# Attention with a maxout feed-forward on one core: the softmax of a chunk overlaps its neighbour, and the feed-forward has three result buffers

## The chip, the core and the metric

The kernel runs on one core of a Trainium2 chip. The metric is the device time of one execution in microseconds (us), as the median of three runs. The core's engines work side by side, each through its own list of instructions in the order of the program: TensorE (PE; its weight loads are PEld), VectorE (DVE), ScalarE (ACT), GpSimd (POOL), and SyncE (SP), which here issues nearly all DMAs. An instruction that waits for another engine holds up everything behind it on its own.

## The reference

Eight batches of 12 heads, 448 tokens, head width 64. Q and K are normalised, attention is computed, the heads are put side by side to rows of 768, and a maxout feed-forward follows. All is float32.

```python
q_n, k_n = rmsnorm(q, g_q), rmsnorm(k, g_k)          # x / sqrt(mean(x*x) + 1e-6) * g
scores = np.matmul(q_n, k_n.transpose(0, 1, 3, 2)) / 8
attn = np.exp(scores - np.max(scores, axis=-1, keepdims=True))
attn = attn / (np.sum(attn, axis=-1, keepdims=True) + 1e-09)
x = np.matmul(attn, v)                               # (8, 12, 448, 64)
x = x.transpose(0, 2, 1, 3).reshape(3584, 768)
h = np.maximum(np.maximum(x @ w1, x @ w2), x @ w3)   # three 768 x 768 weights
out = h @ w_out
```

## The kernel before, in words

To keep float32 accuracy with 16-bit matmuls, every operand is split into an upper float16 part and a lower one (what the upper leaves over), and each product is three matmuls: upper x upper, upper x lower, lower x upper (`TERMS`).

**Groups, chunks, beats.** A group `g` is one batch and two heads: 48 groups, six to a batch. The 448 queries of a group are done in four chunks of 112. The program is written out in beats: a group has 12, `beat(g, i)`, three to a chunk (`c, part = divmod(i, 3)`). Each engine's order is the order in which the beats emit instructions. `later(n, work)` puts work off by n beats; `tick()` at a beat's end emits what is due.

**A chunk of softmax.** `scores` (L469) makes six matmuls into `sc`, a PSUM tile of two banks (one for each head), of which two exist. `softmax` has VectorE take the maximum of each row (L480) and scale it to `nm` (L482); ScalarE then takes the two exponentials in place, with their sums (L486). `upper_weights` makes the reciprocal sums `rs` on VectorE (L496, L500) and the normalised upper parts `pp` on ScalarE (L503). `lower_weights` makes the lower parts on VectorE (L513), which is the last reader of `sc`. `turn_weights` transposes `pp` into `pt` by a DMA (L523). When a group's four chunks are turned, `add_values` (L539) multiplies by V in the next group's beats, and `finish` (L548 on ScalarE, L549 on VectorE) writes the result's two parts `xt`, the feed-forward's input.

**The work around it.** For the groups ahead, beats load Q, K and V (SP), square and sum them (GpSimd L332, VectorE L338), scale them (GpSimd L345 to L383), split them (`upper_rows` on ScalarE L394, `lower_rows` on GpSimd L401) and transpose them (`turn_rows`, L409); V is scaled and split in `scale_v`, `upper_v`, `lower_v`.

**The feed-forward.** When a batch is finished, its feed-forward is queued, and `thirds(n)` takes n thirds from the queue in each beat, by the table `THIRDS`. A third is three matmuls. The first layer (`layer1`, L563, 18 products of six thirds) accumulates into `acc`; `hidden` empties it: the first of three products is copied to `m` (ScalarE L574), the second and third are merged with it by a maximum (VectorE L578), and after the third the result is split into the parts of `ht` (ScalarE L584, VectorE L588). The second layer (`layer2`, L627, six or eight products) accumulates likewise, and `result` (ScalarE L636) copies it to `osb` for the store. All these `acc` come from the pool `ps_m` with two buffers of one bank.

**Decoding.** In the first ten groups the weights arrive as 64-bit floats, and a block of them is decoded every five beats (`prep_block`): ScalarE on `raw` (L171), VectorE on `d_f` (L179, L183, L188, L155), then `largest` finds the block's largest value with two small matmuls into the PSUM tile `marks` (L142, L149) and a maximum `top` (L144) between them; `w_top` (L242) follows from it.

Of the kernel before, what the change touches and what calls it, by code (L numbers as in the profile page):

```python
# [12 lines left out]
ALU = mybir.AluOpType  # L13
# [21 lines left out]
def qknorm_attention_maxout_ffn_kernel(  # L35
# [53 lines left out]
    ps_a = ctx.enter_context(tc.tile_pool(name="ps_a", bufs=1, space=bass.MemoryType.PSUM))  # L89
    ps_m = ctx.enter_context(tc.tile_pool(name="ps_m", bufs=2, space=bass.MemoryType.PSUM))  # L90
    ps_b = ctx.enter_context(tc.tile_pool(name="ps_b", bufs=1, space=bass.MemoryType.PSUM))

# [43 lines left out]

    marks = ps_b.tile([P, 512], F32, name="marks")
    n_marks = [P]

    def largest(column, done):  # L140

        nc.tensor.matmul(marks[0:1, 0:P], column, ident, start=True, stop=True)  # L142
        top = sb.tile([1, 1], F32, name="top", bufs=2)
        nc.vector.tensor_reduce(top, marks[0:1, 0:P], axis=AX, op=ALU.max)  # L144

        def spread():
            at = n_marks[0]
            n_marks[0] += 1
            nc.tensor.matmul(marks[:, at:at + 1], ones, top, start=True, stop=True)  # L149
            done(marks[:, at:at + 1])  # L150

        later(1, spread)

# [64 lines left out]
    def prep_block(n):  # L218
# [47 lines left out]

        later(3, lambda: largest(most, scale))

# [289 lines left out]
    def layer1(b, xs, hs, ft, j, keep):  # L558
        wt = w_sb[:, ft * NJ + j].rearrange("p a (c f) -> p a c f", c=NCT)
        acc = ps_m.tile([P, 512], F32, name="acc", tag="m")  # L560
        for c in range(NCT):
            for n, (wp, xp) in enumerate(TERMS):
                nc.tensor.matmul(  # L563
                    acc[:, :S], wt[:, wp, c], xs[c][:, xp],
                    start=(c == 0 and n == 0), stop=(c == NCT - 1 and n == 2),
                )
            yield
        later(0, lambda: hidden(b, acc, hs, ft, j, keep))

    def hidden(b, acc, hs, ft, j, keep):  # L570
        top = w_top[:, ft, j:j + 1]
# [9 lines left out]
        if j == 2:  # L581
            ht = sb.tile([P, 2, S], F16, name="ht", bufs=6)
            by = h_down[:, ft:ft + 1]
            nc.scalar.activation(ht[:, 0], most, AF.Copy, scale=by)  # L584
            hs.append(ht)

            def lower():
                nc.vector.scalar_tensor_tensor(  # L588
                    out=ht[:, 1], in0=most, scalar=by, in1=ht[:, 0],
                    op0=ALU.mult, op1=ALU.subtract,  # L590
                )
                odd = (b % 2) * LEFT
                nc.gpsimd.tensor_copy(hx[:, ft, :, odd:odd + LEFT], ht[:, :, 3 * P:S])  # L593

            later(1, lower)

# [22 lines left out]
    def layer2(b, hs, tk, half, box):  # L619
# [4 lines left out]
        for f in range(NFT):  # L624
# [6 lines left out]
            yield  # L631
        later(0, lambda: result(b, acc, osb, tk, half))

# [86 lines left out]

    THIRDS = (2, 3, 2, 2, 3, 2, 1, 1, 2, 2, 3, 2)

    def beat(g, i):
        w, n = g - 1, g + 2
        c, part = divmod(i, 3)
        if g < G and part == 0:
            scores(g, c)
            softmax(g, c)
        if g < G and part == 2:
            upper_weights(g, c)  # L730
        if w >= 0 and i == 6:
            add_values(w)
        thirds(THIRDS[i] + (len(queue) > 1 and i % 6 == 4))
        if w >= 0 and i == 8:
            finish(w, x_of[w // NP])
        if w >= 0 and i == 10 and g % NP == 0:
            queue.append(ffn(w // NP, x_of[w // NP]))

        if g + 1 < G:
            if i in (0, 3):  # L740
                upper_rows(g + 1, "kq"[i // 3])
            if i in (1, 4):
                lower_rows(g + 1, "kq"[i // 3])
            if i in (3, 6):
                turn_rows(g + 1, "kq"[i // 3 - 1])

        if n < G:
            if i in (0, 2):
                squares(n, "kq"[i // 2])
            if i in (2, 4):  # L750
                sum_squares(n, "kq"[i // 2 - 1])
            if i == 5:
                inv_rms(n)
            if i == 6:
                scale_k(n)
            if i == 8:
                scale_q(n)
# [4 lines left out]
        if 0 < g < G - 6 and i == 5:  # L762
            load_v(g + 6)
            later(4, lambda: largest_v(g + 6))
        if g == 1 and i == 0:
            bound_v(0)
        if g > 1 and g % NP == 0 and g < G and i == 1:
            bound_v(g // NP)
        if g == 1 and 3 <= i < 6:
            (scale_v, upper_v, lower_v)[i - 3](0)  # L770
        if 0 < g < G and i >= 9:
            (scale_v, upper_v, lower_v)[i - 9](g)

        if g + 3 < G:
            if i == 0:
                load_k(g + 3)
            if i == 2:
                load_q(g + 3)
        if i == 1 and w >= 0:
            turn_weights(w, 3)  # L780
        if g < G and i in (4, 7, 10):
            turn_weights(g, i // 3 - 1)
# [3 lines left out]
        tick()  # L786
        if g < G and part == 2:
            lower_weights(g, c)

    for g in range(G + 1):  # L790
        for i in range(12):
            beat(g, i)
# [35 lines left out]
```

## Time and profile before

| | before |
|---|---|
| median of 3 runs | 1409.9 us (1409.33 to 1411.42) |
| the profiled execution | 1410.49 us, span 1408.7 us, mean granted TensorE clock 0.915 |
| busy, share of the span | TensorE 75%, weight loads 35%, VectorE 62%, ScalarE 51%, GpSimd 51% |

The page counts an engine as busy while one of its compute instructions runs. Where no engine is near its full span, the time goes in waits between them, and the groups of instructions by line say how long each engine stood idle in front of one and what released it. The kernel has three stages: groups with decoding, groups without, and a last stretch in which only the feed-forward is left; shares over the whole span mix them.

### The profile page before, as it was taken

How to read it: one execution, taken by the hardware profiler on the slowest of the kernel's cores; microseconds unless marked ns; L12 is line 12 of the kernel's file. 1: busy time of each engine (PE TensorE's matmuls, PEld its weight loads, DVE VectorE, ACT ScalarE, POOL GpSimd, SP SyncE). 2: the span in 40 equal slices, each digit the busy share in tenths (PEclk: the TensorE clock that was granted, in tenths of full speed). 3: DMA queues.
4: the chain of work that ended last, by engine and by line, in shares of the span. 5: the costliest groups of instructions: out<-in, count | busy, mean ns of one | idle time of the engine just before them, and what ended most of it. 6: DMA issues, size and time to landing. Idle time of an engine off the chain costs nothing. (4 is left out here: it accounts for less than half of the span.)

```text
span 1408.7 us, 18557 instructions
## 1 busy us (share of the span) xinstructions
PE 1050.7 (75%) x6032; PEld 491.6 (35%) x6032; DVE 870.8 (62%) x1741; ACT 722.0 (51%) x1550; POOL 719.8 (51%) x759
## 2 busy tenths in 40 slices
PE   0334434768688888887888988888878989878998
PEld 0111111223234334433343434343433434334554
DVE  4777877778666666566656665666656665656120
ACT  2444445545455555555565565555555555555211
POOL 5575767744355546465564655555465555541000
PEclk9996556888899999999899999999999999999999
DMA  5765656655357565676565566655665657554201
GB/s 138 183 128 145 135 146 152 128 135 126 68 114 147 109 117 113 152 124 114 107 137 123 110 116 146 133 117 108 124 136 113 123 120 145 92 91 68 54 0 45
DMA packets 476800, 164.88 MB, mean 117 GB/s; under 512 B 423200, under 2 KB 472352, under 8 KB 476704
## 3 DMA queue, kind: packets, MB, share of 16 engines
q1 hardware_dynamic: 476176, 163.42, 56.4%
q8 instruction: 47, 0.77, 0.2%
q14 instruction: 49, 0.40, 0.1%
q10 hardware_dynamic: 528, 0.30, 0.1%
HBM read 51.97 MB, written 11.01 MB: 45 GB/s over the span
## 5 line engine op out<-in xcount | busy, mean ns | idle before, releaser
L563 PE MATMUL acc<-xt,w_sb 128*128 128x448 f16 x2592 | 559.7, 370 | 124.2 <-DVE ht L588 58.1
L486 ACT ACTIVATE sc<-sc,nm,down 112x448 f32<-112x448 f32 x384 | 267.8, 697 | 494.4 <-DVE nm L482 444.8
L563 PEld LDWEIGHTS <-w_sb 128*128 128x128 f16 x2592 | 253.0, 101 | 415.0 <-issue 223.7
L513 DVE SCALAR_TENSOR_TENSOR pp<-sc,rs,pp 112x448 f16<-112x448 f32 x384 | 244.7, 679 | 178.6 <-ACT pp L503 175.6
L503 ACT ACTIVATE pp<-sc,rs 112x448 f16<-112x448 f32 x384 | 223.2, 636 | 75.7 <-issue 46.2
L480 DVE TENSOR_REDUCE sc<-sc 112x2 f32<-112x896 f32 x192 | 209.1, 1089 | 8.5 <-PE sc L469 8.4
L469 PE MATMUL sc<-kt,qt 64*112 64x448 f16 x1152 | 171.4, 409 | 36.6 <-DMA qt<-qp 21.9
L627 PE MATMUL acc<-wo_sb,ht 128*128 128x384 f16 x864 | 153.1, 328 | 26.5 <-ACT osb L636 13.7
L401 POOL TENSOR_TENSOR kp<-kn,kp 128x512 f16<-128x512 f32 x48 | 56.8, 1183 | 185.6 <-ACT kp L394 185.6
L401 POOL TENSOR_TENSOR qp<-qn,qp 112x512 f16<-112x512 f32 x47 | 55.5, 1182 | 174.5 <-ACT qp L394 174.5
L539 PE MATMUL av<-pt,vp 128*64 128x448 f16 (+1 forms) x1152 | 136.8, 383 | 6.9 <-POOL vp L456 4.4
L349 POOL TENSOR_TENSOR ri<-ri,half_neg 128x15 f32<-128x15 f32 x48 | 135.4, 2822 | 4.0
L496 DVE TENSOR_SCALAR rs<-sc 112x2 f32<-112x2 f32 x192 | 30.0, 156 | 149.0 <-ACT sc L486 149.0
L627 PEld LDWEIGHTS <-ht 128*128 128x128 f16 x864 | 80.4, 98 | 94.9 <-issue 35.1
L142 PE MATMUL marks<-ident,w_row 128*1 128x128 f32 x48 | 12.6, 359 | 132.1 <-DVE w_row L155 128.6
L469 PEld LDWEIGHTS <-qt 64*112 64x112 f16 x1152 | 66.7, 139 | 117.8 <-issue 68.9
L456 POOL TENSOR_TENSOR vp<-vr,vp 128x448 f16<-128x448 f32 x48 | 51.3, 1069 | 90.2 <-ACT vp L450 89.7
L539 PEld LDWEIGHTS <-vp 128*64 128x64 f16 (+1 forms) x1152 | 61.1, 116 | 80.9 <-issue 47.6
L593 POOL COPY hx<-ht 128x128 f16<-128x128 f16 x48 | 14.0, 292 | 138.1 <-DVE ht L588 120.1
L442 POOL TENSOR_SCALAR vr<-vr,v_up 128x448 f32<-128x448 f32 x48 | 68.4, 1426 | 0.2 <-DVE v_up L435 0.2
L338 DVE TENSOR_REDUCE ss<-sq 128x7 f32<-128x448 f32 x96 | 61.2, 638 | 8.6 <-ACT sq L330 7.6
L366 POOL TENSOR_TENSOR qn<-qn,gain 112x512 f32<-112x512 f32 x47 | 61.1, 1301 | 3.7
(84 smaller groups left out, 1045.0 us busy)
## 6 DMA issues: line engine op xcount, KB each, us to landing
raw<-in_moe_w_dram SPq DMA_DIRECT2D x18, 768.0 KB, 4.5
qr<-in_q_dram SPq DMA_DIRECT2D x47, 224.0 KB, 3.4
kr<-in_k_dram SPq DMA_DIRECT2D x96, 96.0 KB, 2.7
vr<-in_v_dram SPq DMA_DIRECT2D x96, 96.0 KB, 2.7
raw<-in_moe_w_out_dram SPq DMA_DIRECT2D x6, 768.0 KB, 4.4
pt<-pp SPq DMA_TRANSPOSE x192, 3.8
out_dram<-osb SPq DMA_DIRECT2D x8, 336.0 KB, 2.9
out_dram<-osb SPq DMA_DIRECT2D x8, 288.0 KB, 3.3
```

The source lines that it names most:

```text
L338: nc.vector.tensor_reduce(sums[g % 2][:sq.shape[0], at], sq, axis=AX, op=ALU.add)
L349: nc.gpsimd.tensor_tensor(out=ri, in0=ri, in1=half_neg, op=ALU.pow)
L401: on.tensor_tensor(out=parts[:, 1], in0=n, in1=parts[:, 0], op=ALU.subtract)
L442: nc.gpsimd.tensor_scalar(out=vr, in0=vr, scalar1=v_up[:, g // NP:g // NP + 1], scalar2=None, op0=ALU.mult,)
L469: nc.tensor.matmul(sc[:QP, h, :S], qt[rows, qp, c], kt[rows, kp, KEYS[h]], start=n == 0, stop=n == len(TERMS) - 1,)
L480: nc.vector.tensor_reduce(low, sc[:QP, :, :S], axis=AX, op=ALU.max, negate=True)
L486: nc.scalar.activation(sc[:QP, h, :S], sc[:QP, h, :S], AF.Exp, bias=nm[:, h:h + 1], scale=down[:QP], accum_out=sc[:QP, 1, S + 8 + h:S + 9 ...
L503: nc.scalar.activation(pp[:, 0, h], sc[:QP, h, :S], AF.Copy, scale=rs[:, h:h + 1])
L513: nc.vector.scalar_tensor_tensor(out=pp[:, 1, h], in0=sc[:QP, h, :S], scalar=rs[:, h:h + 1], in1=pp[:, 0, h], op0=ALU.mult, op1=ALU.subtract,)
L539: nc.tensor.matmul(av[half, :S], vp[rows, group, vpart], pt[rows, 7 * wp + group], start=u == 0 and n == 0, stop=u == 3 and n == len(TERMS ...
L563: nc.tensor.matmul(acc[:, :S], wt[:, wp, c], xs[c][:, xp], start=(c == 0 and n == 0), stop=(c == NCT - 1 and n == 2),)
L627: nc.tensor.matmul(acc[:, :HW], lhs, wo_sb[:, f, wp, half * HW:(half + 1) * HW], start=(f == 0 and n == 0), stop=(f == NFT - 1 and n == 2),)
```

## The change

- `scores` of a chunk are emitted a beat earlier, in the last beat of the chunk before, ahead of that beat's thirds. In its own first beat the chunk's `softmax` comes first, and `lower_weights` of the chunk before come behind it. `upper_weights` move from the third beat to the second.
- The pool `ps_b` with its one bank goes; `ps_m` has three buffers, and each call of `largest` takes its `marks` tile from them. Its steps `reduce`, `spread` and `done` are now one beat apart.
- `hidden` runs a beat after its product is complete (for the last of a batch at once, as before), the upper part of `ht` a beat after that, and the lower part another; `result` runs a beat later.
- Other work of the beats moves by one or two beats, and one entry of `THIRDS` changes places.

The order on VectorE where the attention runs without decoding. Numbers behind a name tell the tiles of one name apart. Before:

```order
L496 TENSOR_SCALAR rs_5629<-sc_5579 112x2
L500 RECIPROCAL rs_5629<-rs_5629 112x2
L513 SCALAR_TENSOR_TENSOR pp_5632<-sc_5579,rs_5629,pp_5632 112x448 x2
L480 TENSOR_REDUCE sc_5648<-sc_5648 112x2
L482 TENSOR_SCALAR nm_5656<-sc_5648,down_132 112x2
L155 TENSOR_REDUCE v_rows_4685<-vr_5571 128x1
L549 SCALAR_TENSOR_TENSOR xt_5641<-av_5591,xt_5641 128x448
L578 SCALAR_TENSOR_TENSOR acc_5564<-acc_5564,w_top_100,m_5540 128x448
L588 SCALAR_TENSOR_TENSOR ht_5671<-acc_5564,h_down_102,ht_5671 128x448
```

The same chunks in the changed kernel:

```order
L494 TENSOR_SCALAR rs_5691<-sc_5658 112x2
L498 RECIPROCAL rs_5691<-rs_5691 112x2
L577 SCALAR_TENSOR_TENSOR acc_5592<-acc_5592,w_top_96,m_5580 128x448
L547 SCALAR_TENSOR_TENSOR xt_5706<-av_5629,xt_5706 128x448
L478 TENSOR_REDUCE sc_5710<-sc_5710 112x2
L480 TENSOR_SCALAR nm_5729<-sc_5710,down_128 112x2
L511 SCALAR_TENSOR_TENSOR pp_5694<-sc_5658,rs_5691,pp_5694 112x448 x2
L590 SCALAR_TENSOR_TENSOR ht_5709<-acc_5592,h_down_98,ht_5709 128x448
```

Before, the lower parts `pp` of a chunk (tile `sc_5579`) stand ahead of the next chunk's maximum (`sc_5648`); now the maximum of `sc_5710` and its `nm` stand ahead of the lower parts made from `sc_5658`. The two instructions on a third product, into `acc` and then `ht`, stood next to each other and are now four rows apart.

VectorE in a group with decoding; `d_f` is the block being decoded, `w_row`, `marks`, `top` and `w_top` lead to its largest value. Before:

```order
L188 SCALAR_TENSOR_TENSOR d_f_998<-raw_871,d_f_998 128x768
L155 TENSOR_REDUCE w_row_999<-d_f_998 128x1
L144 TENSOR_REDUCE top_1042<-marks_97 1x1
L496 TENSOR_SCALAR rs_1044<-sc_1014 112x2
L500 RECIPROCAL rs_1044<-rs_1044 112x2
L338 TENSOR_REDUCE ss0_87<-sq_1028 128x7
L242 TENSOR_SCALAR w_top_100<-marks_97 128x1
```

The same block in the changed kernel:

```order
L186 SCALAR_TENSOR_TENSOR d_f_997<-raw_871,d_f_997 128x768
L153 TENSOR_REDUCE w_row_998<-d_f_997 128x1
L494 TENSOR_SCALAR rs_1039<-sc_1001 112x2
L498 RECIPROCAL rs_1039<-rs_1039 112x2
L336 TENSOR_REDUCE ss0_84<-sq_1022 128x7
L478 TENSOR_REDUCE sc_1052<-sc_1052 112x2
L480 TENSOR_SCALAR nm_1069<-sc_1052,down_128 112x2
L511 SCALAR_TENSOR_TENSOR pp_1042<-sc_1001,rs_1039,pp_1042 112x448 x2
L143 TENSOR_REDUCE top_1066<-marks_1064 1x1
```

Before, `top` stood right behind `w_row`, which TensorE first has to turn. Now the sums, the next chunk's maximum and the lower parts stand between the two.

The diff, cut to its core:

```diff
-    ps_m = ctx.enter_context(tc.tile_pool(name="ps_m", bufs=2, space=bass.MemoryType.PSUM))
-    ps_b = ctx.enter_context(tc.tile_pool(name="ps_b", bufs=1, space=bass.MemoryType.PSUM))
+    ps_m = ctx.enter_context(tc.tile_pool(name="ps_m", bufs=3, space=bass.MemoryType.PSUM))
...
-    marks = ps_b.tile([P, 512], F32, name="marks")
-    n_marks = [P]
-
     def largest(column, done):
 
+        marks = ps_m.tile([P, 512], F32, name="marks", tag="m")
         nc.tensor.matmul(marks[0:1, 0:P], column, ident, start=True, stop=True)
         top = sb.tile([1, 1], F32, name="top", bufs=2)
-        nc.vector.tensor_reduce(top, marks[0:1, 0:P], axis=AX, op=ALU.max)
+
+        def reduce():
+            nc.vector.tensor_reduce(top, marks[0:1, 0:P], axis=AX, op=ALU.max)
 
         def spread():
-            at = n_marks[0]
-            n_marks[0] += 1
-            nc.tensor.matmul(marks[:, at:at + 1], ones, top, start=True, stop=True)
-            done(marks[:, at:at + 1])
-
-        later(1, spread)
+            nc.tensor.matmul(marks[:, P:P + 1], ones, top, start=True, stop=True)
+
+        later(1, reduce)
+        later(2, spread)
+        later(3, lambda: done(marks[:, P:P + 1]))
...
-        later(3, lambda: largest(most, scale))
+        later(4, lambda: largest(most, scale))
...
-        later(0, lambda: hidden(b, acc, hs, ft, j, keep))
-
-    def hidden(b, acc, hs, ft, j, keep):
+        gap = 0 if ft == NFT - 1 and j == NJ - 1 else 1
+        later(gap, lambda: hidden(b, acc, hs, ft, j, keep, gap))
+
+    def hidden(b, acc, hs, ft, j, keep, gap):
...
-            nc.scalar.activation(ht[:, 0], most, AF.Copy, scale=by)
             hs.append(ht)
+
+            def upper():
+                nc.scalar.activation(ht[:, 0], most, AF.Copy, scale=by)
+                later(1, lower)
...
-            later(1, lower)
+            later(gap, upper)
...
-        later(0, lambda: result(b, acc, osb, tk, half))
+        later(1, lambda: result(b, acc, osb, tk, half))
...
-    THIRDS = (2, 3, 2, 2, 3, 2, 1, 1, 2, 2, 3, 2)
+    THIRDS = (2, 3, 2, 2, 3, 2, 2, 0, 2, 2, 3, 2)
...
-        if g < G and part == 0:
-            scores(g, c)
-            softmax(g, c)
-        if g < G and part == 2:
+        k = 4 * g + c
+        if part == 0:
+            if g < G:
+                softmax(g, c)
+            if 0 < k <= 4 * G:
+                lower_weights(*divmod(k - 1, 4))
+        if part == 1 and g < G:
             upper_weights(g, c)
-        if w >= 0 and i == 6:
+        if part == 2 and k + 1 < 4 * G:
+            scores(*divmod(k + 1, 4))
+        if w >= 0 and i == 7:
             add_values(w)
         thirds(THIRDS[i] + (len(queue) > 1 and i % 6 == 4))
-        if w >= 0 and i == 8:
+        if w >= 0 and i == 10:
             finish(w, x_of[w // NP])
...
-        if 0 < g < G and i >= 9:
-            (scale_v, upper_v, lower_v)[i - 9](g)
+        if 0 < g < G and i == 9:
+            scale_v(g)
+        if 0 < g < G and i == 11:
+            upper_v(g)
+        if 0 < w and i == 0:
+            lower_v(w)
...
-            if i == 2:
+            if i == 1:
                 load_q(g + 3)
-        if i == 1 and w >= 0:
+        if i == 2 and w >= 0:
             turn_weights(w, 3)
-        if g < G and i in (4, 7, 10):
+        if g < G and i in (5, 8, 11):
             turn_weights(g, i // 3 - 1)
...
-        if g < G and part == 2:
-            lower_weights(g, c)
-
+
+    scores(0, 0)
     for g in range(G + 1):
```

Left out above: `upper_rows`, `lower_rows`, `turn_rows`, `squares`, `sum_squares`, `inv_rms`, `scale_k` and the first group's `bound_v` and `scale_v` stand one or two beats elsewhere.

## Rows read from the trace of the kernel before

**Rows 1.** Busy time by stretch: engines (instructions), granted clock, DMA share, GB/s.

```profile
125.00:158.00 33.00, 11.53 (x56) 4.84 (x56) 25.32 (x47) 17.25 (x34) 22.09 (x20) 0.55 0.59 133
...
400.00:1300.00 900.00, 757.18 (x4513) 354.70 (x4511) 560.75 (x1160) 513.87 (x1137) 484.76 (x531) 0.95 0.61 120
```

**Rows 2.** Timeline of ScalarE, line 548: start, us, engine, line, tiles, count.

```profile
82.12 0.54 ACT L548 ACTIVATE xt<-av 128x448 f16<-128x448 f32 x1
...
388.67 0.54 ACT L548 ACTIVATE xt<-av 128x448 f16<-128x448 f32 x1
...
1299.69 0.54 ACT L548 ACTIVATE xt<-av 128x448 f16<-128x448 f32 x1
```

**Rows 3.** Groups by line, 400 to 1300 us: busy, mean ns | idle before, releasers.

```profile
L486 ACT ACTIVATE sc<-sc,nm,down 112x448 f32<-112x448 f32 x292 | 203.6, 697 | 362.6 <-DVE nm L482 327.0 <-DVE v_down L431 13.2 <-DVE v_most L428 13.2
...
L513 DVE SCALAR_TENSOR_TENSOR pp<-sc,rs,pp 112x448 f16<-112x448 f32 x293 | 186.9, 679 | 158.3 <-ACT pp L503 155.3 <-DMA kr<-in_k_dram 1.7 <-DMA pt<-pp 1.3
...
L563 PE MATMUL acc<-xt,w_sb 128*128 128x448 f16 x1944 | 418.1, 368 | 104.5 <-DVE ht L588 56.0 <-ACT m L574 31.4 <-ACT osb L636 10.4
```

**Rows 4.** Timeline of one chunk, ScalarE and VectorE.

```profile
705.89 0.70 ACT L486 ACTIVATE sc<-sc,nm,down 112x448 f32<-112x448 f32 x1 [2.14 <-DVE nm L482]
...
707.48 0.16 DVE L496 TENSOR_SCALAR rs<-sc 112x2 f32<-112x2 f32 x1 [1.09 <-ACT sc L486]
...
707.92 1.16 ACT L503 ACTIVATE pp<-sc,rs 112x448 f16<-112x448 f32 x2 [0.48 <-ACT sc L486]
...
709.11 1.28 DVE L513 SCALAR_TENSOR_TENSOR pp<-sc,rs,pp 112x448 f16<-112x448 f32 x2 [1.27 <-ACT pp L503]
710.30 1.09 DVE L480 TENSOR_REDUCE sc<-sc 112x2 f32<-112x896 f32 x1
711.43 0.22 DVE L482 TENSOR_SCALAR nm<-sc,down 112x2 f32<-112x2 f32 x1
...
711.74 0.70 ACT L486 ACTIVATE sc<-sc,nm,down 112x448 f32<-112x448 f32 x1 [2.23 <-DVE nm L482]
```

**Rows 5.** Timeline of TensorE in stretches without a wait.

```profile
702.69 0.78 PE L469 MATMUL sc<-kt,qt 64*112 64x448 f16 x6
703.40 2.58 PE L539 MATMUL av<-pt,vp 128*64 128x448 f16 x24
705.91 2.12 PE L627 MATMUL acc<-wo_sb,ht 128*128 128x384 f16 x12
707.96 0.78 PE L469 MATMUL sc<-kt,qt 64*112 64x448 f16 x6
...
1275.36 4.14 PE L563 MATMUL acc<-xt,w_sb 128*128 128x448 f16 x21
1279.43 0.40 PE L469 MATMUL sc<-kt,qt 64*112 64x448 f16 x2
```

**Rows 6.** TensorE behind waits: timeline, and one stretch: busy (count), granted clock, DMA share, GB/s.

```profile
958.59 3.56 PE L563 MATMUL acc<-xt,w_sb 128*128 128x448 f16 x18 [0.99 <-DVE m L578]
...
966.17 6.51 PE L563 MATMUL acc<-xt,w_sb 128*128 128x448 f16 x18 [3.31 <-DVE ht L588]
...
967.50:970.00 2.50, 2.50 (x8) 0.50 0.49 91
...
1304.57 7.47 PE L627 MATMUL acc<-wo_sb,ht 128*128 128x384 f16 x45 [3.14 <-ACT osb L636]
```

**Rows 7.** Groups by line on VectorE, 82 to 247 us.

```profile
L513 DVE SCALAR_TENSOR_TENSOR pp<-sc,rs,pp 112x448 f16<-112x448 f32 x42 | 26.7, 676 | 9.1 <-ACT pp L503 9.1
...
L179 DVE TENSOR_SCALAR d_f<-raw 128x768 uint32<-128x768 uint32 x12 | 10.6, 880 | 11.9 <-ACT raw L171 11.9
...
L144 DVE TENSOR_REDUCE top<-marks 1x1 f32<-1x128 f32 x13 | 3.6, 275 | 3.3 <-PE marks L142 3.1
...
L242 DVE TENSOR_SCALAR w_top<-marks 128x1 f32<-128x1 f32 x12 | 1.9, 155 | 5.4 <-PE marks L149 5.2
```

**Rows 8.** DMA issues of the page: size or none, median us to landing.

```profile
pt<-pp SPq DMA_TRANSPOSE x192, 3.8
```

More of the change, by code (lines that the diff above doesn't have):

```diff
@@ L725, in beat @@
         c, part = divmod(i, 3)
-        if g < G and part == 0:
-            scores(g, c)
-            softmax(g, c)
-        if g < G and part == 2:
+        k = 4 * g + c
[5 more added lines that the diff above has]
+        if part == 1 and g < G:
             upper_weights(g, c)
-        if w >= 0 and i == 6:
+        if part == 2 and k + 1 < 4 * G:
+            scores(*divmod(k + 1, 4))
+        if w >= 0 and i == 7:
             add_values(w)
         thirds(THIRDS[i] + (len(queue) > 1 and i % 6 == 4))
-        if w >= 0 and i == 8:
+        if w >= 0 and i == 10:
             finish(w, x_of[w // NP])
-        if w >= 0 and i == 10 and g % NP == 0:
-            queue.append(ffn(w // NP, x_of[w // NP]))
+            if g % NP == 0:
+                queue.append(ffn(w // NP, x_of[w // NP]))
         if g + 1 < G:
-            if i in (0, 3):
[L741 to L752, printed above, removed]
+            if i in (1, 2):
+                upper_rows(g + 1, "kq"[i - 1])
+            if i in (2, 4):
+                lower_rows(g + 1, "kq"[i // 2 - 1])
+            if i in (4, 6):
+                turn_rows(g + 1, "kq"[i // 2 - 2])
+        if n < G:
+            if i in (0, 3):
+                squares(n, "kq"[i // 3])
+            if i in (2, 5):
+                sum_squares(n, "kq"[i // 3])
+            if i == 6:
                 inv_rms(n)
-            if i == 6:
+            if i == 7:
                 scale_k(n)
@@ L764, in beat @@
             later(4, lambda: largest_v(g + 6))
-        if g == 1 and i == 0:
+        if g == 0 and i == 9:
             bound_v(0)
+        if g == 1 and 3 <= i < 6:
+            (scale_v, upper_v, lower_v)[i - 3](0)
         if g > 1 and g % NP == 0 and g < G and i == 1:
             bound_v(g // NP)
-        if g == 1 and 3 <= i < 6:
-            (scale_v, upper_v, lower_v)[i - 3](0)
-        if 0 < g < G and i >= 9:
-            (scale_v, upper_v, lower_v)[i - 9](g)
+        if 0 < g < G and i == 9:
[4 more added lines that the diff above has]
+            lower_v(w)
         if g + 3 < G:
```

## The prediction

> **What bounds the kernel now.** Start with the table by stage [rows 1] and the ends of the groups [rows 2]. A group is a batch and a pair of heads, 48 in all; ScalarE's line 548 runs once in each. The first such end is at 82.12 us, the tenth at 388.67 and the 47th at 1299.69. So nine groups in which the weights are still decoded take 306.55 us, 34.06 each, and 37 groups after them 911.02 us, 24.62 each. The remaining 109 us belong to TensorE almost alone. Between 400 and 1300 us (36.6 groups) TensorE is busy 757.18 of 900 us, VectorE 560.75, ScalarE 513.87, GpSimd 484.76, and the DMA engines at a share of 0.61 [rows 1]. No engine is full, so look for a chain.
>
> The groups of instructions of that stretch name it [rows 3]: ScalarE stood idle 362.6 us before the exponentials of line 486, mostly for `nm`, the scaled maximum that VectorE makes. VectorE stood idle 158.3 us before the lower parts of line 513, for ScalarE's upper parts. Each waits for the other. The timeline of one chunk shows the circle [rows 4]: exponentials from 705.89, reciprocal sums from 707.48, upper parts from 707.92, lower parts from 709.11, the next chunk's maximum from 710.30, its `nm` from 711.43, its exponentials from 711.74. That is 5.85 us for a chunk with every step behind the last. Four chunks make 23.40; the measured 24.62 is 5.2% more, which is what other work in between costs.
>
> TensorE's 142.8 us of idle time are a consequence: matmuls of line 563 alone waited 104.5 us [rows 3], mostly until VectorE or ScalarE, themselves late, had emptied one of the two buffers `acc`.
>
> **The maximum ahead of the lower parts.** In the new order of VectorE a chunk's `sc` is reduced and `nm` is made before the previous chunk's lower parts. The numbers of instructions do not change; every duration stays. What leaves the circle is the lower parts (709.11 to 710.30, 1.19 us), the maximum (1.13) and `nm` with its hand-over (0.31) [rows 4]: 2.63 us of the 5.85. ScalarE can go from upper parts straight to the next exponentials. Left in its circle are 705.89 to 707.92 and the upper parts, 3.2 us; with a group's other casts and copies ScalarE has 513.87 / 36.6 = 14.1 us of work a group, and VectorE 15.3 [rows 1]. The attention could therefore go at some 16 us a group. What is late next is TensorE.
>
> Its content of a group follows from starts of uninterrupted stretches [rows 5]. 21 matmuls of line 563 take 1279.43 - 1275.36 = 4.07 us, so a third (three matmuls) 0.581. Twelve of line 627 take 707.96 - 705.91 = 2.05, a third 0.512. Scores take 703.40 - 702.69 = 0.71 us a chunk, the values 705.91 - 703.40 = 2.51 a group. A batch has 108 thirds of the first layer and 36 or 48 of the second; the 25 thirds that `THIRDS` gives a group, unchanged in sum, are then 18 and 7. So 18 x 0.581 + 7 x 0.512 + 4 x 0.71 + 2.51 = 19.40 us at full clock. Something will still rub. I give the new bound the same 5.2% that the old one shows: 20.41. The gain is 37 x (24.62 - 20.41) = 155.8 us. The ends: 19.40 (no friction, gain 193) and, at the other side, 24.62 or more, for the reasons under the rivals.
>
> Does the new order hold TensorE up? `scores` of chunk k+1 now wait for the lower parts of k-1, since only two `sc` exist, and those come behind the maximum of k. Counted from the end of the scores of k: an estimated 0.1 for the hand-over, then 1.13, 0.2 and 1.19 make 2.6 us. TensorE has seven thirds in between, 4.07 us. Slack 1.4 us. Queued behind that wait are all further thirds. The upper parts of k end about 4.8 us after its scores (0.1 + 1.13 + 0.31 + 2.03 + 1.16), just about when the scores of k+1 end, and the lower parts want them 1.4 us later.
>
> **Three result buffers, later emptying.** `ps_m` gets the bank that `marks` had, and `marks` now takes a turn among the three. A buffer is wanted again after 12 thirds and two scores, 8.4 us, instead of after six and one. The longest holder is the third product of a tile: maximum one beat later, upper part another, lower part another, at most four beats of 20.41 / 12 = 1.7 us, so 6.8. The extra bank hides the extra beats with 1.6 us to spare; gone, it would cost TensorE about today's idle time, 142.8 / 36.6 = 3.9 us a group. The last tile keeps a gap of 0, so the second layer waits no longer than now. Moving results of the second layer by a beat lies inside the same 8.4 us. These edits I cost at nothing.
>
> **Beats that move.** Squares, sums, scaling, row splits, `bound_v`, `scale_v`, `upper_v` and `lower_v` are shifted by one or two beats. The same instructions stay on GpSimd, 484.76 / 36.6 = 13.3 us a group, and on the SP queue. There the transposition of a group's last chunk is now issued behind the next group's loads of K and Q: landing takes a median 3.8 us [rows 8], its lower parts end 2.6 us after the first scores of the group, and the values follow two rounds of scores and 18 thirds' time later, at 11.9 us. That leaves 5 us for the loads in front. The DMA engines' 0.61 x 24.62 = 15.0 us a group fit into 20.4. Cost nothing; if the queue were late, up to those 5 us are cover.
>
> **The stage with decoding.** Here the bound is VectorE: 25.32 us busy in 33 [rows 1], and TensorE has little to do at a granted clock of 0.55. Its idle time over five groups [rows 7]: before the lower parts 9.1 us, before `top` 3.3, before `w_top` 5.4, before `d_f` 11.9. The first three, 17.8 us, go, as the maxima stand in front and `reduce`, `spread` and `done` are now a beat apart: 3.6 us a group. The `d_f` wait for ScalarE's pass over `raw` stays. A new wait comes: the sums need the exponentials, 1.9 us after `nm` (0.31 + 1.59), and the lower parts cover 1.4, leaving 0.5 where no decode work follows, two chunks in a group, so 1.0. Net 2.6 us in nine groups, 23, and 2 for the start. Bounds: all idle time gone, 7.7 x 9 = 69; a loss of 1 us a group, 9, if `marks` among the buffers hold TensorE's queue. I take 25.
>
> **The tail.** TensorE works through 96 instead of 90 matmuls behind the last scores (1.0 us more) and loses the 3.14 us wait at 1304.57 [rows 6]. 2 us less.
>
> **The sum.** The profiled execution took 1410.5 us (span 1408.7), 0.6 above the median of the runs. 1410.5 - 155.8 - 25 - 2 = 1228 us.
>
> **A place where the clock matters.** After a wait of 3.31 us the next 18 matmuls took 6.51 us, at a granted clock of 0.50, the lower level of 1.2 GHz; after a wait of 0.99 us the same 18 took 3.56 [rows 6]. The mean granted clock of the steady stage is 0.95, which is why TensorE's busy time, 757.18 / 36.6 = 20.7, is above the content of 19.40. I expect the long waits to go and the clock to stay at 2.4 GHz.
>
> The Trainium skill, "TensorE: Matmul & The Clock Gate", section "A second HAM failure mode: psum-queue depth-cycling", says that a kernel that cycles through PSUM buffers with small idle gaps can make the gate swing and lose throughput. The 0.99 us gap at full clock speaks against it, the 3.31 us one for it; by that rule the rival on the clock, 1279 us, would be the forecast.
>
> **Rivals.**
> (a) The clock keeps falling: small waits at each change of buffer remain. Then a group needs the 20.7 us of today's busy time, with friction 21.8: gain 105, time 1279. For it: the 0.95; against: three buffers instead of two.
> (b) The later emptying eats the third buffer: half of today's TensorE waits stay, 20.7 + 1.95 = 22.7 us a group, gain 71, time 1312. For it: 1.6 us of spare on an estimate; against: the third buffer doubles the time until a buffer is wanted again, from 4.2 us (six thirds and one round of scores) to 8.4.
> (c) The change does not do what it says: the next scores stand behind seven thirds, the maximum waits for them, and the lower parts wait behind it. For it: VectorE takes its instructions in the order written. Against: the 1.4 us of slack. The group stays at 24.6, time 1408 to 1412.
> (d) Slower. The scores wait for the lower parts of k-1 long enough that the clock falls. Such a stall costs 3.31 us and then 6.51 - 3.56 = 2.95, together 6.3 us. One in each group makes 20.4 + 6.3 = 26.7: 37 x 2.1 = 77 more, 25 and 2 less, 1460. It decides from 0.8 of a stall a group on (20.4 + 0.8 x 6.3 = 25.4 eats the other gains too). It needs lower parts 4.7 us late against the slack of 1.4.
>
> **How the numbers follow.** Forecast 0.64, (a) 0.15, (b) 0.12, (c) 0.03, (d) 0.06. The low end takes 19.40 a group and 40 us of the decode stage: 1410.5 - 193 - 40 - 2 = 1175. The high end reaches through (a) to (b): 1310. Left out are (c), (d) and a little on each side. A change of under 0.2% counts as none, since this kernel's measurement tells no less. Faster 0.91 (forecast, a, b), same 0.03, slower 0.06.
>
> **What would show it.** Right: ends of groups some 20.4 us apart; ScalarE's wait for `nm` down from 10 us a group to under 3; TensorE busy over 93% of the steady stage at a clock near 1.00, its waits for `ht` and `m` nearly gone; groups with decoding near 31 us. Wrong: TensorE waiting in `scores` for the lower parts of line 511 (c, d), for `acc` (b), a clock under 0.97 in the steady stage (a), or the maximum waiting for scores with TensorE idle.

## The result and the profile after

The changed kernel takes 1212.47 us (median of 4 runs, 1211.85 to 1213.33), the kernel before beside it 1409.62: a ratio of 0.8601, 95% interval 0.8586 to 0.8616. The forecast was 1228, its range 1175 to 1310. Lines from 155 to 563 are two lower in the changed kernel (line 486 of before is 484, 513 is 511, 548 is 546); behind that, 574 is 573, 578 is 577, and 584, 588, 627 and 636 are two higher.

First the table by stage, as in [rows 1]: TensorE's busy time comes first, then the loading of weights, VectorE, ScalarE, GpSimd, then the granted clock, the DMA share and GB/s. The first line is a stretch of the decoding, the second the steady stage, the third a single group of it.

```profile
110.00:142.00 32.00, 10.66 (x58) 4.94 (x58) 26.50 (x50) 18.84 (x39) 23.61 (x21) 0.61 0.83 185
...
400.00:1100.00 700.00, 682.47 (x4276) 329.62 (x4276) 525.35 (x1106) 491.40 (x1082) 457.93 (x503) 1.00 0.79 147
...
440.80:461.00 20.20, 20.20 (x126) 9.52 (x124) 15.96 (x34) 13.86 (x31) 13.84 (x16) 1.00 0.78 143
```

TensorE is busy 97.5% of the steady stage at a clock of 1.00; before it was 84% at 0.95 [rows 1]. There are whole groups in which it does not stop at all. The ends of the groups, as in [rows 2]:

```profile
78.80 0.56 ACT L546 ACTIVATE xt<-av 128x448 f16<-128x448 f32 x1
...
360.39 0.54 ACT L546 ACTIVATE xt<-av 128x448 f16<-128x448 f32 x1
...
1107.83 0.54 ACT L546 ACTIVATE xt<-av 128x448 f16<-128x448 f32 x1
```

The first end is 3.3 us earlier, nine groups with decoding take 281.59 in place of 306.55 (25.0 less, 31.29 each), 37 steady ones 747.44 in place of 911.02 (163.6 less, 20.20 each), and behind the 47th end 103.3 us are left in place of 109.0 (5.7 less; line 546 now stands two beats of 1.7 us later in its group, which by itself takes 3.4 us out of this last part and puts as much into the parts ahead of the tenth end). Together that is the 197.6 us between the spans of 1408.7 and 1211.1.

The groups of instructions of the steady stage, as in [rows 3] (busy time, mean ns of one, idle time before them and what ended it):

```profile
L561 PE MATMUL acc<-xt,w_sb 128*128 128x448 f16 x1944 | 386.5, 353 | 0.0
L484 ACT ACTIVATE sc<-sc,nm,down 112x448 f32<-112x448 f32 x279 | 194.6, 697 | 156.5 <-DVE nm L480 151.9
...
L511 DVE SCALAR_TENSOR_TENSOR pp<-sc,rs,pp 112x448 f16<-112x448 f32 x280 | 177.3, 675 | 0.2 <-issue 0.2
...
L478 DVE TENSOR_REDUCE sc<-sc 112x2 f32<-112x896 f32 x139 | 151.9, 1093 | 54.1 <-PE sc L467 53.8
L467 PE MATMUL sc<-kt,qt 64*112 64x448 f16 x834 | 107.7, 363 | 8.8 <-DVE pp L511 5.8 <-DMA qt<-qp 2.7
L629 PE MATMUL acc<-wo_sb,ht 128*128 128x384 f16 x552 | 101.1, 334 | 9.7 <-DVE rs L494 5.4 <-ACT osb L638 4.2
```

The same 1944 matmuls of the first layer waited 104.5 us before and 0.0 now, and took 386.5 us in place of 418.1. The lower parts' wait for the upper ones, 158.3 us, is 0.2. ScalarE still waits for `nm`; VectorE, which makes it, waits longest for the scores (54.1), and TensorE, which makes those, hardly waits at all. One chunk, as in [rows 4], ScalarE and VectorE, with TensorE's next scores last:

```profile
608.25 1.16 ACT L501 ACTIVATE pp<-sc,rs 112x448 f16<-112x448 f32 x2 [0.48 <-ACT sc L484]
...
608.70 1.10 DVE L478 TENSOR_REDUCE sc<-sc 112x2 f32<-112x896 f32 x1
609.84 0.22 DVE L480 TENSOR_SCALAR nm<-sc,down 112x2 f32<-112x2 f32 x1
609.98 1.27 DVE L511 SCALAR_TENSOR_TENSOR pp<-sc,rs,pp 112x448 f16<-112x448 f32 x2
...
610.84 0.71 ACT L484 ACTIVATE sc<-sc,nm,down 112x448 f32<-112x448 f32 x1
...
612.67 0.78 PE L467 MATMUL sc<-kt,qt 64*112 64x448 f16 x6
```

The next chunk's maximum (608.70) runs beside the upper parts (608.25), and its exponentials (610.84) beside the lower parts (609.98). The scores that need the `sc` of these lower parts start at 612.67, 1.4 us after the lower parts' end at 611.25: the slack that was forecast.

### The profile page after: what moved, and what is told of

It reads as the page before. It is cut to its first block, busy times and chain, and to the rows that moved or that the text cites. A ratio compares the mean times of both kernels' runs of the same rounds, so it can differ in the third digit from the quotient of the medians.

```text
span 1211.1 us, 18488 instructions
## 1 busy us (share of the span) xinstructions
PE 1005.5 (83%) x6032; PEld 482.9 (40%) x6032; DVE 848.8 (70%) x1741; ACT 722.1 (60%) x1550; POOL 714.9 (59%) x759
## 5 line engine op out<-in xcount | busy, mean ns | idle before, releaser
L561 PE MATMUL acc<-xt,w_sb 128*128 128x448 f16 x2592 | 525.4, 358 | 15.1 <-ACT m L573 12.3
L561 PEld LDWEIGHTS <-w_sb 128*128 128x128 f16 x2592 | 245.4, 99 | 279.2 <-issue 71.5
L467 PE MATMUL sc<-kt,qt 64*112 64x448 f16 x1152 | 164.2, 394 | 95.2 <-DVE pp L511 53.3
L454 POOL TENSOR_TENSOR vp<-vr,vp 128x448 f16<-128x448 f32 x48 | 49.6, 1032 | 86.1 <-ACT vp L448 82.1
L547 DVE SCALAR_TENSOR_TENSOR xt<-av,xt 128x448 f16<-128x448 f32 x48 | 29.9, 624 | 72.7 <-ACT xt L546 72.7
(84 smaller groups left out, 1015.0 us busy)
```

The source lines that it names most:

```text
L467: nc.tensor.matmul(sc[:QP, h, :S], qt[rows, qp, c], kt[rows, kp, KEYS[h]], start=n == 0, stop=n == len(TERMS) - 1,)
L561: nc.tensor.matmul(acc[:, :S], wt[:, wp, c], xs[c][:, xp], start=(c == 0 and n == 0), stop=(c == NCT - 1 and n == 2),)
```

## The experiments

Four times for each profiled execution, from its ends of groups: the start is the first end, the decoding the nine groups to the tenth, then 37 steady groups (and one of them), and what lies behind the 47th.

| kernel | start | decoding | steady | one | behind | median |
|---|---|---|---|---|---|---|
| before | 82.1 | 306.6 | 911.0 | 24.62 | 109.0 | 1409.62 |
| changed | 78.8 | 281.6 | 747.4 | 20.20 | 103.3 | 1212.47 |
| e1 lower parts first | 84.4 | 305.5 | 916.7 | 24.78 | 104.9 | 1412.21 |
| e3 order alone | 82.9 | 291.0 | 739.6 | 19.99 | 103.3 | 1220.43 |
| e5 buffers alone | 79.1 | 296.5 | 921.5 | 24.90 | 108.3 | 1408.88 |
| e4 emptied at once | 78.0 | 264.3 | 740.7 | 20.02 | 103.2 | 1187.97 |
| e10 first layer at once | 77.5 | 264.2 | 742.7 | 20.07 | 103.2 | 1190.09 |
| e9 e4 with the tiles side by side | 77.3 | 264.4 | 738.0 | 19.95 | 103.2 | 1184.72 |
| e8 tiles side by side | 77.2 | 281.7 | 742.2 | 20.06 | 103.3 | 1205.66 |
| e11 changed, one more on VectorE | 82.8 | 291.2 | 793.7 | 21.45 | 103.2 | 1274.91 |
| e12 before, one more on VectorE | 82.7 | 330.0 | 1015.0 | 27.43 | 111.2 | 1541.03 |
| e6 changed, two products | 78.9 | 277.9 | 719.3 | 19.44 | 82.8 | 1162.71 |
| e7 before, two products | 81.6 | 302.7 | 910.3 | 24.60 | 89.1 | 1385.84 |

**The two lines that matter.** e1 is the changed kernel with two calls exchanged:

```diff
         if part == 0:
-            if g < G:
-                softmax(g, c)
             if 0 < k <= 4 * G:
                 lower_weights(*divmod(k - 1, 4))
+            if g < G:
+                softmax(g, c)
```

> The changed kernel with one exchange: in a chunk's first beat the lower parts of the chunk before are emitted ahead of the chunk's maximum again; buffers and all beats stay. Theory A (the order of maximum and lower parts on VectorE set the pace): the circle of 5.85 us a chunk is back, a group takes 23.4 to 24.6 us instead of 20.2, so 37 x 3.2 to 4.4 more, 1330 to 1375 us, and ScalarE's wait for nm is back near 10 us a group. Theory B (the third buffer freed TensorE, the order matters little): 1212 to 1240 us.

e1 takes 1412.21 us, ratio 1.0002 (0.9993 to 1.0012): with everything else of the change in place, nothing is gained. The timeline of ScalarE and VectorE in e1 shows the old circle:

```profile
703.88 0.70 ACT L484 ACTIVATE sc<-sc,nm,down 112x448 f32<-112x448 f32 x1 [1.86 <-DVE nm L480]
...
705.91 1.16 ACT L501 ACTIVATE pp<-sc,rs 112x448 f16<-112x448 f32 x2 [0.48 <-ACT sc L484]
707.11 1.28 DVE L511 SCALAR_TENSOR_TENSOR pp<-sc,rs,pp 112x448 f16<-112x448 f32 x2 [1.28 <-ACT pp L501]
708.30 1.09 DVE L478 TENSOR_REDUCE sc<-sc 112x2 f32<-112x896 f32 x1
...
709.74 0.70 ACT L484 ACTIVATE sc<-sc,nm,down 112x448 f32<-112x448 f32 x1 [2.66 <-DVE nm L480]
```

709.74 - 703.88 = 5.86 us, against 5.85 before [rows 4]. That is more time than theory A gave back to the circle (1330 to 1375 us): scores that come earlier and the third buffer do not shorten the circle at all, as VectorE takes the lower parts, which wait for the upper ones, before the maximum. Whether the exchange would bring as much without the scores a beat earlier was not tried.

**The order without the buffers, the buffers without the order.** e3 is the changed kernel with `ps_m` at two buffers, `marks` in a bank of its own, `reduce` and `spread` at the old beats, and both layers emptied in the same beat. e5 is the changed kernel with the old `beat`, so the old order, and the old `THIRDS`.

```diff
 e3:
-    ps_m = ctx.enter_context(tc.tile_pool(name="ps_m", bufs=3, space=bass.MemoryType.PSUM))
+    ps_m = ctx.enter_context(tc.tile_pool(name="ps_m", bufs=2, space=bass.MemoryType.PSUM))
+    ps_b = ctx.enter_context(tc.tile_pool(name="ps_b", bufs=1, space=bass.MemoryType.PSUM))
...
-        later(1, reduce)
-        later(2, spread)
-        later(3, lambda: done(marks[:, P:P + 1]))
+        later(1, spread)
...
+        gap = 0
...
+        later(0, lambda: result(b, acc, osb, tk, half))
 e5:
-            if g < G:
-                softmax(g, c)
-            if 0 < k <= 4 * G:
-                lower_weights(*divmod(k - 1, 4))
...
+        if g < G and part == 0:
+            scores(g, c)
+            softmax(g, c)
```

> The changed kernel with the buffers as before: two for the products, marks in a bank of its own, products emptied in the beat in which they end, largest as before; the new order of the softmax stays. Theory A: the circle stays open and TensorE's waits for the two buffers cost part of the gain, a group of 21.5 to 23 us, 1260 to 1315 us. Theory B: without the third buffer most of the gain is lost, 1350 us or more. Theory C (the order alone is the whole gain, buffers are hidden): 1210 to 1225 us.

> The kernel before with only the buffers of the change: three for products and marks, later emptying, largest in separate beats (and the first bound_v three beats earlier, so that its value is there in time); the softmax order stays. Theory A: the circle of 5.85 us a chunk still sets the pace, 24.0 to 24.6 us a group, 1385 to 1412 us, with TensorE's waits moved from acc to the scores or simply shorter and more idle elsewhere. Theory B: TensorE's 3.9 us of waits a group go, 1265 to 1330 us.

e3 takes 1220.43 us, ratio 0.8645 (0.8628 to 0.8662), e5 1408.88, ratio 0.9982 (0.9972 to 0.9991). So the order alone brings nearly everything that the change brings, and two buffers are enough for a TensorE that hardly stops (busy 685.82 of 700 us from 400 us on). e5 shows both signs of the rest: 10 us less in decoding, 10 more in the steady stage, where TensorE waits up to 5.2 us at a time for a `marks` behind the second layer's results (21.8 us in all). The buffers are not worth nothing, though: e3 and e4 below differ only in the third buffer and the separate steps of `largest`, and start and decoding take 373.9 us in the one and 342.3 in the other. VectorE's waits before `top` and `w_top`, 5.9 and 12.6 us there in e3, are 0.0 in e4. How much of it is the buffer's and how much the steps' was not tried, nor were two buffers with the later emptying.

**The later emptying.** e4 takes only this away from the changed kernel, e10 only the first of its two lines:

```diff
-        gap = 0 if ft == NFT - 1 and j == NJ - 1 else 1
+        gap = 0
...
-        later(1, lambda: result(b, acc, osb, tk, half))
+        later(0, lambda: result(b, acc, osb, tk, half))
```

> The changed kernel with three buffers, but each product emptied in the beat in which it ends and result in the same beat, as before. Theory A1 (the later emptying only uses time that the third buffer gives; it could be left out): 1205 to 1222 us. Theory A2 (emptying in the same beat makes VectorE and ScalarE wait for TensorE's last matmul in front of the next maximum): a wait of about 1 us at each of 4.2 products a group, part of it in the slack of 1.4 us, 1230 to 1290 us, with idle time of VectorE before L577 from TensorE.

> The changed kernel with one line back: the first layer's results are emptied in the beat in which their last product is issued, the second layer's still a beat later. The kernel with both back took 1187.97 us, 24.5 less than the changed one; of that 17.3 us lie in the nine decode groups (264.3 against 281.6) and 6.7 in the 37 steady ones (20.02 against 20.20 each). Theory E: it is the first layer's delay. From 253 us on, where the first batch's first layer has begun and the weights' marks still take a third of the same three buffers, TensorE waits 21 us in the changed kernel for a result buffer (acc and marks behind ACT m and DVE ht). Then 1188 to 1196 us. Rival F: it is the second layer's delay, whose buffer is wanted sooner (its products come at 18 a buffer): then 1205 to 1212.

e4 takes 1187.97 us, ratio 0.8415 (0.8401 to 0.8429): lower than either theory said, and 24.5 less than the changed kernel. e10 takes 1190.09, ratio 0.8432 (0.8421 to 0.8444), which is theory E: the first layer's delay costs nearly all of it. The place is the last three groups of the decoding: 34.8, 32.0 and 38.4 us in the changed kernel, 25.9, 28.7 and 32.6 in e10. What TensorE waits for there, from 253 to 360 us of the changed kernel (us in total, times, longest):

```profile
PE acc L561 <- ACT m L573: 11.8, 2, 6.1
...
PE marks L139 <- ACT m L573: 5.9, 1, 5.9
PE marks L139 <- DVE ht L590: 3.5, 1, 3.5
```

And in the same stretch of e10:

```profile
PE acc L561 <- DVE ht L590: 2.2, 1, 2.2
PE marks L139 <- DVE ht L590: 1.5, 1, 1.5
```

21.2 us of waits for one of the three buffers become 3.7 in these rows (0.4 more stands behind `m`, and TensorE's waits for the lower parts grow from 1.8 to 7.4 us). A beat there is some 35 / 12 = 2.9 us, and `marks` holds one of the three buffers for three beats. The longest wait of the changed kernel, TensorE and then ScalarE:

```profile
298.13 0.38 PE L139 MATMUL marks<-ident,w_row 128*1 128x128 f32 x2
...
305.27 3.85 PE L561 MATMUL acc<-xt,w_sb 128*128 128x448 f16 x12 [6.08 <-ACT m L573]
...
304.56 0.66 ACT L573 ACTIVATE m<-acc,w_top 128x448 f32<-128x448 f32 x1
```

Two buffers are taken: by the `marks` of 298.13, last read at 309.46, and by a third product whose last reader, line 590, starts at 304.73. The one left holds a first product, and TensorE stops until ScalarE, a beat late and behind its other work, has copied that to `m`. 17.7 of the 21.2 us end with this copy, 5.9 of them with a `marks` as the one that waits. The waits are not all of the loss. The three groups in the changed kernel and in e10 (engines, granted clock, DMA share, GB/s, as in [rows 1]):

```profile
255.22:360.39 105.17, 76.93 (x398) 33.57 (x399) 73.64 (x139) 51.37 (x105) 47.06 (x49) 0.84 0.53 112
```

```profile
254.64:341.71 87.07, 69.96 (x392) 31.59 (x391) 72.50 (x138) 51.41 (x105) 47.66 (x48) 0.93 0.66 134
```

With the longer waits the granted clock is 0.84 in place of 0.93, and nearly as many matmuls take 7 us more.

**The change of layers.** e9 is e4, and e8 the changed kernel, each with the first two result tiles of the second layer filled side by side, so that the last `ht` is wanted later:

```diff
-        for tk in range(3 + b % 2):
+        first = [layer2(b, hs, 0, half, box) for half in range(NH)]
+        for half in range(NH):
+            for f in range(NFT - 1):
+                yield next(first[half])
+        for half in range(NH):
+            yield from first[half]
+        for tk in range(1, 3 + b % 2):
```

> The changed kernel with both layers' results emptied in the same beat (1187.97 us), and with the first two result buffers of the second layer filled side by side: five sixths of each, and only then the two sixths that read the last hidden tile. Theory G: what TensorE still waits at the start of the second layer (4.3 us in all before its matmuls, 8 batches) goes: 1183 to 1187 us. Rival H: two result buffers half filled hold up the third one, and a wait of some 1.5 us a batch comes: 1195 to 1205.

> The changed kernel, with only the order of the second layer's first two result buffers changed, as in the kernel above. In the changed kernel TensorE waits 1.81 us there in a batch (10.8 in all before these matmuls), and in two of the batches the granted clock falls to .86 to .93 behind it and the group takes 22.3 to 22.6 us in place of 20.2. Theory G: the wait and the fall go, 10 to 14 us: 1198 to 1203. Rival H: the same time goes to a wait elsewhere, since the two buffers are held longer: 1209 to 1216.

e9 takes 1184.72 us, ratio 0.8395 (0.8381 to 0.8409), inside theory G's bounds and the lowest time here; against e4 the intervals overlap, against the changed kernel they do not. e8 takes 1205.66, ratio 0.8544 (0.8532 to 0.8557): less than the changed kernel, but 6.8 us and not the 10 to 14 of theory G. The two groups of 22.56 and 22.28 us in the changed kernel are gone (e8's longest steady one behind the first is 20.66), and some of the wait went to the scores: 5.8 us behind the lower parts in 700 us became 9.7 in 690. The last lines on TensorE's waits, e8 from 400 to 1090 us and then e9 from 400 to 1070:

```profile
PE sc L467 <- DVE pp L511: 9.7, 15, 1.1
PE acc L629 <- ACT osb L638: 4.9, 7, 1.0
```

```profile
PE sc L467 <- DVE pp L511: 7.9, 16, 1.2
PE sc L467 <- DMA qt<-qp: 0.2, 1, 0.2
```

**Who sets the steady group now.** e11 and e12 add one instruction of 0.68 us a chunk to VectorE, in the changed kernel and in that of before; e6 and e7 leave out one of the three products of the first layer, so their hidden layer is less exact.

```diff
 e11, e12:  in lower_weights
-        for h in range(2):
+        for h in (0, 0, 1):
 e6, e7:  in layer1
-            for n, (wp, xp) in enumerate(TERMS):
+            for n, (wp, xp) in enumerate(TERMS[:2]):
```

> The changed kernel, in which VectorE computes the lower part of the first half of each chunk's weights twice (one more instruction of .675 us a chunk, 192 in all; the output stays the same). Theory T: TensorE sets the steady groups, and VectorE has 15.2 us of work in the 20.2 of a group, 17.9 with the four more: no change there; in the nine decode groups, where VectorE is busy .85 of the time, 36 times .675, 24 us, can come out: 1212 to 1240 us. Theory U: the circle of softmax, only shorter, still sets the steady group: then 148 times .675 come to it, 100 us, and the 24 of the decode groups: 1310 to 1340.

> The kernel before, in which VectorE computes the lower part of the first half of each chunk's weights twice (.675 us more a chunk). Theory T: here the instruction stands in the circle of one chunk (5.85 us of 5.85), so each of 148 steady chunks grows by it, 100 us, and the decode groups by 5 to 24: 1510 to 1535 us. Theory V: the steady group of before was set by TensorE at 19.4 us of work and by waits of its own that have nothing to do with the circle: then 1410 to 1435.

> The changed kernel without one of the three products of the first layer (the lower part of the weights by the upper of the values or the reverse is left out, so the hidden layer is less exact): 864 matmuls of .194 us fewer, 3.5 us a group on average. Theory T: TensorE sets the steady groups, and they shorten until another engine sets them (VectorE has 15.2 us of work, ScalarE 14.2): 37 times 2.5 to 3.5 us, and up to 21 in the tail: 1075 to 1125 us. Theory U: the shortened circle sets them: 1195 to 1213 (only the tail shortens).

> The kernel before without the same product of the first layer. Theory T: the circle of softmax sets the steady groups, TensorE has time over: nothing but the tail shortens, 1385 to 1410 us. Theory V: TensorE and its own waits set them: 37 times 3 us less, 1280 to 1310.

Before is as theory T has it, with e12 6 us above its bounds. e12 takes 1541.03 us, ratio 1.0927 (1.0909 to 1.0945), 131 more, and 192 x 0.68 is 131: each added instruction lies on the path (a steady group grows by 2.81, a chunk by 0.70). e7 takes 1385.84, ratio 0.9826 (0.9812 to 0.9841): 108 matmuls of each batch are gone, the steady group stays at 24.60, and 19.9 of the 24 us come from behind the 47th end.

After is between the two theories. e11 takes 1274.91, ratio 0.9035 (0.9013 to 0.9057); its steady group grows by 1.25 us where theory T had nothing and U had 2.7. e6 takes 1162.71, ratio 0.8241 (0.822 to 0.8262); its steady group loses 0.76 where T had at least 2.5. Both name what comes next. TensorE's longest wait in e6, 400 to 1050 us, is for the lower parts that free a `sc`:

```profile
PE sc L467 <- DVE pp L511: 61.6, 52, 2.6
```

How that comes about shows in VectorE and TensorE of e11, one after the other:

```profile
633.31 0.62 DVE L547 SCALAR_TENSOR_TENSOR xt<-av,xt 128x448 f16<-128x448 f32 x1 [1.12 <-ACT xt L546]
633.86 1.09 DVE L478 TENSOR_REDUCE sc<-sc 112x2 f32<-112x896 f32 x1
634.98 0.22 DVE L480 TENSOR_SCALAR nm<-sc,down 112x2 f32<-112x2 f32 x1
635.12 1.98 DVE L511 SCALAR_TENSOR_TENSOR pp<-sc,rs,pp 112x448 f16<-112x448 f32 x3
```

```profile
631.52 0.78 PE L467 MATMUL sc<-kt,qt 64*112 64x448 f16 x6
632.23 4.15 PE L561 MATMUL acc<-xt,w_sb 128*128 128x448 f16 x21
637.15 0.77 PE L467 MATMUL sc<-kt,qt 64*112 64x448 f16 x6 [0.78 <-DVE pp L511]
```

The scores are there at 632.3, but VectorE stands at line 547 and begins the maximum at 633.86; the lower parts end at 637.1, and the next scores start at 637.15, 0.78 us after TensorE had run out of thirds. Line 547 itself had waited 1.12 us for ScalarE. So scores, maximum, lower parts, next scores form a second circle, with whatever VectorE has in between. In the changed kernel TensorE's work hides it with little to spare; take a sixth of that work away (e6), and TensorE, busy 564.83 of 650 us, waits mostly there, at 19.4 us a group. That this circle alone sets those 19.4 is not shown.

## Why the prediction was right, and where it was not

- **The circle, and what leaves it.** Right. e1 puts two calls back and the 5.86 us are back; e12 lengthens it and all of it shows; e7 gives TensorE less work and the steady group does not move.
- **TensorE as the next bound, 20.41 a group.** Right in kind: busy 97.5%, clock 1.00. The size was 20.20: busy time is 682.47 / 34.65 groups = 19.70 against the 19.40 of content, and 0.5 is idle. The friction of 5.2% was taken from a bound of another kind; it was 4.1%. Worth 163.6 us in place of 155.8.
- **"The attention could go at some 16 us a group."** Not reached. It added up ScalarE's and VectorE's work and left out that scores wait for a free `sc`. e6 gets to 19.44, with 61.6 us of such waits in 650. It did not touch the forecast, since TensorE's 20.2 lie above it, but only by 0.8.
- **ScalarE's wait for `nm` under 3 us a group.** Wrong: 151.9 / 34.65 = 4.4. An engine that is no longer the bound waits for the one that is; its idle time was no sign of the step.
- **Scores' slack of 1.4 us.** Right in the chunk shown; in the whole steady stage TensorE waited there 5.8 us, so rival (d) did not come, and neither did (c).
- **The three buffers and the later emptying "cost at nothing".** Wrong by 22 to 24 us. The 1.7 us a beat are of the steady stage, and there the cost is only 0.1 to 0.2 us a group (e10, e4). In the last three groups of the decoding a beat lasts 2.9 us, so that the four beats of a third product are 11.7 us, over the 8.4 reckoned until a buffer is wanted again, and a `marks` holds or wants another buffer beside it. What TensorE then waits for is mostly not the longest holder of the working but the first product's copy `m`, a beat late (17.7 of 21.2 us). The working named `marks` among the buffers only as a bound of 1 us a group. Rival (b) had the mechanism, but put it in the steady stage.
- **Decoding and start, 25 us.** The sum was near (28.3, or some 32 counted to the same place in the program), but by luck, as two errors cancel: without the later emptying the decoding gains 42.3 us (e10), with it 25.0. The waits named did go. From 79 to 223 us VectorE's lines that answer to [rows 7]:

```profile
L511 DVE SCALAR_TENSOR_TENSOR pp<-sc,rs,pp 112x448 f16<-112x448 f32 x40 | 25.3, 675 | 0.0
L177 DVE TENSOR_SCALAR d_f<-raw 128x768 uint32<-128x768 uint32 x13 | 10.2, 786 | 7.5 <-ACT raw L169 6.4 <-POOL w_sb L251 0.5 <-DMA kr<-in_k_dram 0.5
L143 DVE TENSOR_REDUCE top<-marks 1x1 f32<-1x128 f32 x13 | 3.4, 265 | 0.0
L494 DVE TENSOR_SCALAR rs<-sc 112x2 f32<-112x2 f32 x20 | 3.1, 155 | 5.7 <-ACT sc L484 5.7
L240 DVE TENSOR_SCALAR w_top<-marks 128x1 f32<-128x1 f32 x12 | 1.8, 146 | 0.0
...
L547 DVE SCALAR_TENSOR_TENSOR xt<-av,xt 128x448 f16<-128x448 f32 x5 | 3.1, 621 | 6.1 <-ACT xt L546 6.1
```

  The 9.1, 3.3 and 5.4 us before the lower parts, `top` and `w_top` are all 0.0. The wait for the sums went from 2.0 to 5.7 us in five groups, 0.7 more in each against the 1.0 forecast. The working missed three things: the wait before `d_f`, which was to stay, fell from 11.9 to 7.5, the three passes over `d_f` (lines 177, 181 and 186) took 4.3 us less, and VectorE now waits 6.1 us for ScalarE's half of `xt`, where it waited 0.0. These five groups take 144.0 us in place of 164.0; the last four, with the buffers, 137.6 in place of 142.5.
- **The waits of the second layer, "no longer than now".** Right in length: before, TensorE waited 1.86 us for the last `ht` in four batches (7.4 us in 900, line 627 behind line 588), now 1.81 in three. But before, the softmax set the pace; now TensorE does, and the wait costs: e8 shows 6.8 us for it and what follows.
- **The tail, 2 us.** Right: 5.7 less behind the 47th end, 3.4 of it by the place of line 546, and TensorE runs there without a wait.
- **The clock, rival (a).** It did not come: 1.00. Gaps of up to 0.84 us before scores and results left it there. The rule weighed in the prediction (the Trainium skill, "TensorE: Matmul & The Clock Gate", section "A second HAM failure mode: psum-queue depth-cycling") has the gate swing where TensorE idles briefly between groups of matmuls; from 400 us on the trace agrees with it only behind the 1.81 us waits, and there not each time (below).

## What to carry to other kernels

When a chain runs round through an engine that takes its work in order, look at what stands ahead of the step that closes it: two calls exchanged were worth 200 us here (e1 against the changed kernel), a third buffer nothing in the steady stage (e3 and e4, 19.99 and 20.02 us a group), though with the separate steps of `largest` it brought 26.7 us of the decoding. Work out how long a buffer is held in the stage with the longest beats, not in the one with the most groups, and count every other tile that takes its turn in the same pool. When a bound gives way, the next two may lie close together; taking away work of the one (e6) shows where the other is.

## What the runs showed of the hardware

The same wait had two outcomes. In the changed kernel TensorE waits 1.81 us at 731.93 and, in another batch, at 491.47, at the change of layers, until VectorE has made the last `ht` (the rows name `rs`, which it runs right behind). Here are the matmuls behind each, and the stretch 736.0 to 738.4 (busy, count, granted clock, DMA share, GB/s):

```profile
493.28 0.34 PE L629 MATMUL acc<-wo_sb,ht 128*128 128x384 f16 x1 [1.81 <-DVE rs L494]
...
494.25 2.12 PE L629 MATMUL acc<-wo_sb,ht 128*128 128x384 f16 x12
...
733.74 0.34 PE L629 MATMUL acc<-wo_sb,ht 128*128 128x384 f16 x1 [1.81 <-DVE rs L494]
...
734.72 3.80 PE L629 MATMUL acc<-wo_sb,ht 128*128 128x384 f16 x12
```

```profile
736.00:738.40 2.40, 2.40 (x9) 0.53 0.90 170
```

Twelve matmuls took 2.12 us behind the first and 3.80 behind the second, at a granted clock near the lower level of 1.2 GHz. A third such wait, up to 976.16, went like that of 731.93: clock 0.50 from 978 to 980. A longer one, 2.71 us up to 401.82 for a DMA, left the clock at 1.00. So the length of the wait alone does not decide it here, and why one of three equal waits was followed by no fall stays open. And a clock that falls need not cost: with a product less (e7) the steady stage of before had a mean granted clock of 0.91 in place of 0.95, and its groups took 24.60 us as before: TensorE had 224 us of idle time in 890, against 142.8 in 900 before, and the slower matmuls came out of that.
